# Strassen's products in layer 2, crossbar transposes and a new load order in a fused attention and MLP kernel

## The chip, the cores and the metric

The kernel runs on one core of a Trainium2 chip. The metric is device time in microseconds (us); every number for a kernel is the median of its executions unless it is called a range. A "span" is a little shorter than the time: it goes from the first to the last instruction of the one execution that was profiled. All readings of engines come from such profiles. PE is the matmul engine, DVE the vector engine, ACT the scalar engine, POOL is GpSimd, SP is the sync engine, which here issues nearly all DMAs, one after another (144 of 155 in the trace before).

## The reference

```python
# q, k, v: (8 batches, 8 heads, 576 rows, 64); w_ch1: (512, 2048); w_ch2: (2048, 512)
scores = scale * q @ k.T                      # window: 0 <= row - column < 64
attn = exp(scores - max) / (sum + 1e-9)       # masked
x = concat_heads(attn @ v)                    # (8, 576, 512)
xn = (x - mean) / sqrt(var + 1e-6) * g_ln     # layer norm (LN) of each row
out = x + relu(xn @ w_ch1) @ w_ch2            # float32
```

The kernel works in groups of 512 rows. Groups 0 to 7 are the first 512 rows of each batch; group 8 collects the last 64 rows of all eight batches, two batches to a block of 128; these four blocks are called tails. A group has four blocks of 128 rows.

## The kernel before

Each group is a list of units: sixteen units of layer 1 (four matmuls of 512 columns each), then sixteen of layer 2. Between the units of group g the kernel places, by slot number, the attention of batch g+1, the casts of batch g+2 and so on. Each engine gets its own instructions in this program order.

```python
    def l1(hc):                                    # layer 1: one unit
        ...
        for kc in range(NKC):                      # 4 matmuls of 512 columns
            nc.tensor.matmul(out=hps, lhsT=w1g[:, kc, 128*hc:128*(hc+1)], rhs=zT[g][:, kc, :], ...)
        nc.scalar.activation(out=hrT[:, hc, :], in_=hps, func=AF.Relu, ...)
    def l2(kb, part):                              # layer 2: one unit
        for hc in range(4*part, 4*part+4):         # 4 matmuls of 512 columns
            nc.tensor.matmul(out=ch[kb], lhsT=hrT[:, hc, 128*kb:128*(kb+1)], rhs=w2s[:, hc, :], ...)
        if part == 3: add_out(kb)                  # DVE: ch * rstd + x into osb, then the store
...
    def b_step(g, kb):                             # value matmuls, then on DVE: x, statistics, and
        nc.vector.scalar_tensor_tensor(out=z, in0=xn, scalar=mvg[...], in1=gB,   # z = (x - mean) * g
                                       op0=ALU.subtract, op1=ALU.mult)
    def zt_step(g, kb):                            # four PE transposes of z, one ACT copy into zT
...
        if g > 1 and b < B:                        # b = g + 1
            for j in range(4):
                at(1 + 6*j, s_mm, b, j); at(2 + 6*j, s_mask, b, j)
                at(7 + 6*j, b_step, b, j); at(min(13 + 6*j, 29), zt_step, b, j)
```

The softmax here doesn't subtract the row's maximum and nothing guards it: scores larger than these inputs give would overflow.

Of the kernel before, what the change touches and what calls it, by code (L numbers as in the profile page):

```python
# [20 lines left out]
def kernel(  # L21
# [10 lines left out]
    nc = tc.nc  # L32
# [8 lines left out]
    EPS = 1e-6  # L41
    scale = 1.0 / (D ** 0.5)
# [6 lines left out]
    p_pt = ctx.enter_context(tc.tile_pool(name="ppt", bufs=6))  # L49
    p_xn = ctx.enter_context(tc.tile_pool(name="pxn", bufs=8))  # L50
# [5 lines left out]
    ps_t = ctx.enter_context(tc.tile_pool(name="pst", bufs=2, space=PSUM))  # L56
# [7 lines left out]
    gB = p_const.tile([128, DM], FP32, tag="gB", name="gB")  # L64
    w1g = p_const.tile([128, NKC, HID], FP16, tag="w1g", name="w1g")
    w2s = p_const.tile([128, NHC, DM], FP16, tag="w2s", name="w2s")

# [20 lines left out]
    def load_tail(i):  # L88
        tq = p_in.tile([128, H, D], FP32, tag="tq32", name=f"tq32_{i}", bufs=1)
        tk = p_in.tile([128, 2, H, D], FP32, tag="qk32_1", name=f"tk32_{i}")  # L90
        tv = p_in.tile([128, 2, H, D], FP32, tag="qk32_0", name=f"tv32_{i}")
        tail32[i] = (tq, tk, tv)
        for r in range(2):
            b = 2 * i + r
            nc.sync.dma_start(out=tq[64 * r:64 * r + 64], in_=q[b, :, SM:S, :].rearrange("h s d -> s h d"))
            nc.sync.dma_start(out=tk[:, r], in_=k[b, :, S - 128:S, :].rearrange("h s d -> s h d"))
            nc.sync.dma_start(out=tv[:, r], in_=v[b, :, S - 128:S, :].rearrange("h s d -> s h d"))
# [13 lines left out]
    def cast_qk(b, half):  # L111
        for x in range(2):
# [60 lines left out]
    def w1_cast(i, eng):  # L173
        q2, pr = divmod(i, 2)
        t = wst.pop(("w1", i))
        dst = w1g[:, 2 * pr:2 * pr + 2, (HID // 4) * q2:(HID // 4) * (q2 + 1)]
        if eng == "act":
            nc.scalar.copy(out=dst, in_=t)
        else:
            nc.gpsimd.tensor_copy(out=dst, in_=t)  # L180
# [14 lines left out]

    def evac(x, out, in_):
# [5 lines left out]
    def t_main(b, x, half, eng=None):  # L202
        src = qk16.pop((b, x, half))
        j = 2 if b < 2 else 4
        tp = ps_t.tile([128, 8, 128], FP16, tag="tp", name=f"tp_{b}_{x}_{half}")
# [10 lines left out]
    def t_tail(i):  # L216
        q16, k16 = tail16.pop(i)
        tqk = (p_qkt.tile([128, NHP, 128], FP16, tag="tqT", name=f"tqT_{i}", bufs=1),
               p_qkt.tile([128, 2, NHP, 128], FP16, tag="tkT", name=f"tkT_{i}", bufs=1))
        tailT[i] = tqk  # L220
        tp = ps_t.tile([128, 2, NHP, 128], FP16, tag="tp", name=f"tpk_{i}")
        for r in range(2):
            for hp in range(NHP):
                nc.tensor.transpose(out=tp[:, r, hp, :], in_=k16[:, r, 2 * hp:2 * hp + 2, :], identity=ident16)
        evac(0, tqk[1], tp)
        tp = ps_t.tile([128, NHP, 128], FP16, tag="tp", name=f"tpq_{i}")
        for hp in range(NHP):
            nc.tensor.transpose(out=tp[:, hp, :], in_=q16[:, 2 * hp:2 * hp + 2, :], identity=ident16)
        evac(0, tqk[0], tp)

    def s_mm(g, j, pe_mask=False):
# [11 lines left out]
        for hp in range(NHP):  # L243
            for iw in range(2):
                for par in range(2):
# [4 lines left out]
                    else:  # L250
                        w = 2 * j + iw
                        lhsT = qkT[g][1][rows, hp, 64 * w:64 * w + 128]
                        rhs = qkT[g][0][rows, hp, 64 * w:64 * w + 64]
                    nc.tensor.matmul(out=sc[par][:, hp, iw, :], lhsT=lhsT, rhs=rhs,
                                     start=not pe_mask, stop=True, skip_group_check=pe_mask)
        for par in range(2):
            nc.scalar.activation(out=pt[:, par], in_=sc[par], func=AF.Exp, bias=0.0, scale=scale)
# [8 lines left out]
    def b_step(g, kb):  # L266
        kblk = f"{g}_{kb}"
        sfx, nb = ("r", 4) if g == NGRP - 1 else ("", None)
        xn = p_xn.tile([128, H, D], FP32, tag="xn" + sfx, name=f"xn_{kblk}", bufs=nb)
        x_norm[(g, kb)] = xn  # L270
# [17 lines left out]
        nc.vector.bn_stats(out=stats, in_=xn[:, :, :].rearrange("p h d -> p (h d)"))  # L288
        if g not in mvg:
            mvg[g] = p_grp.tile([128, 4, 2], FP32, tag="mvg" + sfx, name=f"mvg_{g}", bufs=1 if sfx else 2)  # L290
        nc.vector.bn_aggr(out=mvg[g][:, kb, :], in_=stats)
        z = p_blk.tile([128, DM], FP16, tag="z", name=f"z_{kblk}")
        zsd[(g, kb)] = z
        nc.vector.scalar_tensor_tensor(
            out=z, in0=xn[:, :, :].rearrange("p h d -> p (h d)"), scalar=mvg[g][:, kb, 0:1], in1=gB,
            op0=ALU.subtract, op1=ALU.mult,
        )

    def zt_step(g, kb, eng="act"):
# [4 lines left out]
        ztp = ps_t.tile([128, NKC, 128], FP16, tag="tp", name=f"ztp_{g}_{kb}")  # L304
# [8 lines left out]
    def group_stats(g, eng=nc.gpsimd):  # L313
        rstd[g] = p_grp.tile([128, 4], FP32, tag="rstdg", name=f"rstdg_{g}")
        rs = rstd[g]
        mv = mvg[g]
        tmp = p_grp.tile([128, 3, 4], FP32, tag="rstmp", name=f"rstmp_{g}")
        ve, hv, ab = tmp[:, 0], tmp[:, 1], tmp[:, 2]
        nc.vector.tensor_scalar(out=ve, in0=mv[:, :, 1], scalar1=EPS, scalar2=None, op0=ALU.add)
        nc.vector.tensor_scalar(  # L320
            out=ab.bitcast(I32), in0=ve.bitcast(I32), scalar1=1, scalar2=None,
            op0=ALU.logical_shift_right,
        )
        nc.vector.tensor_tensor(out=rs[:, :].bitcast(I32), in0=magt[:, :].bitcast(I32),  # L324
                                in1=ab.bitcast(I32), op=ALU.subtract)
        eng.tensor_scalar(out=hv, in0=mv[:, :, 1], scalar1=0.5, scalar2=0.5 * EPS,
                                op0=ALU.mult, op1=ALU.add)
# [6 lines left out]
    def mlp_units(g, split=0, two=False):  # L334
        hrT = p_hrt.tile([128, NHC, 512], FP16, tag="hrT", name=f"hrT_{g}")
        units = []
# [23 lines left out]
        def add_out(kb):  # L360
            o = p_blk.tile([128, DM], FP32, tag="osb", name=f"osb_{g}_{kb}")
            nc.vector.scalar_tensor_tensor(  # L362
                out=o, in0=ch[kb], scalar=rstd[g][:, kb:kb + 1],
                in1=x_norm[(g, kb)][:, :, :].rearrange("p h d -> p (h d)"), op0=ALU.mult, op1=ALU.add,
            )
            if g == NGRP - 1:
                for r in range(2):
                    nc.sync.dma_start(out=out[2 * kb + r, SM:S, :], in_=o[64 * r:64 * r + 64])
            else:
                nc.sync.dma_start(out=out[g, 128 * kb:128 * kb + 128, :], in_=o)  # L370
# [28 lines left out]
        for half in range(2):  # L399
            for i in range(split // 2):  # L400
                units.append(lambda half=half, i=i: l1_half(half, i))
        for hc in range(split, NHC):
# [4 lines left out]
        for kb in range(2 if two else 0, 4):  # L407
            for part in range(4):
                units.append(lambda kb=kb, part=part: l2(kb, part))
        return units  # L410
# [5 lines left out]
    ones1 = p_const.tile([1, 128], FP32, tag="ones1", name="ones1")  # L416
# [8 lines left out]
    nc.vector.memset(ones1, 1.0)  # L425
    nc.gpsimd.affine_select(
# [7 lines left out]
    nc.vector.tensor_scalar(out=mbias, in0=mask, scalar1=-1.0, scalar2=30000.0, op0=ALU.add, op1=ALU.mult)  # L434
    for b in range(2):
# [9 lines left out]
    for i in range(8):  # L445
        w1_cast(i, "pool")

    warm = ps_mm.tile([128, 512], FP32, tag="mm", name="warm")

    def keep_clock(n):  # L450
        m = mbias[:, :]
        mb = bass.AP(tensor=m.tensor, offset=m.offset, ap=[m.ap[0], [0, 8], m.ap[1]])
        for _ in range(n):
            nc.tensor.matmul(out=warm[:, :].rearrange("p (a i) -> p a i", i=64), lhsT=ident16, rhs=mb,  # L454
                             start=True, stop=True)


    keep_clock(4)
    gps = ps_mm.tile([128, DM], FP32, tag="mm", name="gps")
    nc.tensor.matmul(out=gps, lhsT=ones1, rhs=g1, start=True, stop=True)  # L460
    nc.vector.tensor_copy(out=gB, in_=gps)
# [51 lines left out]
    for g in range(NGRP):  # L513
        units = mlp_units(g, (8, 16)[g] if g < 2 else 0, g == 0)
# [6 lines left out]
        if g == 0:  # L521
# [3 lines left out]
            at(4, group_stats, 0, nc.vector)  # L525
# [6 lines left out]
            at(16, s_mm, 1, 0, True)  # L532
            at(17, s_mm, 1, 1, True)
# [9 lines left out]
            at(29, s_mm, 1, 2, True)  # L543
            at(30, s_mm, 1, 3, True)
            at(30, load_v, 2, 0, 4)
            at(31, b_step, 1, 2)
        if g == 1:
# [3 lines left out]
            at(2, zt_step, 1, 2)  # L551
            at(5, zt_step, 1, 3)
# [8 lines left out]
            for c in range(4):  # L561
                at(7, vB_cur, 2, c, 1)
                if c < 3:
                    at(7, vB_prev, 2, c, 1)
            for j in range(4):
                at(9 + 4 * j, s_mm, 2, j)
                at(10 + 4 * j, s_mask, 2, j)
                at(13 + 4 * j, b_step, 2, j)
                at(17 + 4 * j, zt_step, 2, j)
        if g > 1 and b < B:  # L570
            at(0, alloc_vB, b)
            at(0, make_vB, b)
            for j in range(4):
                at(1 + 6 * j, s_mm, b, j)
                at(2 + 6 * j, s_mask, b, j)
                at(7 + 6 * j, b_step, b, j)
                at(min(13 + 6 * j, 29), zt_step, b, j)
        if g > 0:
            at(13, group_stats, g)
        for n, i in enumerate(TAILS.get(g, ())):  # L580
            at(3 + 12 * n, t_tail, i)
            at(5 + 12 * n, s_mm, NGRP - 1, i)
            at(6 + 12 * n, s_mask, NGRP - 1, i)
            at(10 + 12 * n, b_step, NGRP - 1, i)
            at(16 + 12 * n, zt_step, NGRP - 1, i)
        if 0 < g and b + 1 < B:
# [56 lines left out]
```

## Time and profile before

| | before |
|---|---|
| time, median of 4 | 336.12 us (335.85 to 336.39) |
| profiled span | 334.6 us |
| PE busy | 96% |
| DVE, ACT, POOL busy | 50%, 52%, 34% |
| DMA, the hardware queue's share of 16 engines | 54.1% |

From the page of the kernel before: engine totals, then four of the lines that cut the span into 40 slices (digits are the busy tenths of a slice; PEclk is the granted matmul clock in tenths of full speed), and the engine shares of the chain that ended last.

```profile
PE 322.8 (96%) x2887; PEld 171.9 (51%) x2887; DVE 168.0 (50%) x307; ACT 175.5 (52%) x292; POOL 114.8 (34%) x198
PE   7988999999999999999999999999999999999994
POOL 7577655413800195008400780058004103201000
PEclk9999999999999999999999999999999999999999
DMA  8999999976239557950369188903460155020022
PE 85%; DVE 4%; SPq 4%; DMA 2%; ACT 1%; issue 1%; POOL 1%; ACTq 0%
```

PE is busy for 80% or more of every slice from the second to the last but one, the clock row shows no reduction, and the last chain is PE work. So PE work that goes away is time that goes away, as long as nothing else makes PE wait. The waits of PE, longest first (total, times, longest one):

```profile
PE warm L454 <- DVE mbias L434: 2.3, 1, 2.3
PE hph_1_0_574 L377 <- ACT zT_375 L309: 0.9, 1, 0.9
PE hph_0_1_1011 L377 <- ACT hrT_992 L382: 0.7, 1, 0.7
```

A busy PE is not the price of a matmul, because matmuls overlap: in this trace one of 512 columns in layer 2 lasts 380 ns. The distance from one matmul's start to the next is: 216 ns at 512 columns, 109 ns at 256, 56 ns for a 128-column transpose.

### The profile page before, as it was taken

Reading aid. Unit: us, or ns where it says so; the run is one execution under the profiler, and the core shown is the slowest. Engines: PE = TensorE matmul, PEld = TensorE weight load, DVE = VectorE, ACT = ScalarE, POOL = GpSimd, SP = SyncE. Lnnn points to the kernel's source line nnn. Section 1 sums busy time; section 2 is a strip of 40 time slices with the busy share of each in tenths; the row PEclk is TensorE's granted clock in tenths of the full one; section 3 lists DMA queues with packets and bytes.
Section 4 is the critical chain, followed back from the end, with each engine's and each line's share of the span. In section 5 each row is a group of like instructions: output and inputs, shape, how many; then the busy total and the mean of one; then the engine's idle time right before and its main releaser. Section 6 shows DMA issues by size and latency. Waiting matters only on the chain.

```text
span 334.6 us, 6996 instructions
## 1 busy us (share of the span) xinstructions
PE 322.8 (96%) x2887; PEld 171.9 (51%) x2887; DVE 168.0 (50%) x307; ACT 175.5 (52%) x292; POOL 114.8 (34%) x198
## 2 busy tenths in 40 slices
PE   7988999999999999999999999999999999999994
PEld 2556445786554455545545554456445444444441
DVE  1795682777933565286415751767235714241011
ACT  2586515485267644974468356763675157505500
POOL 7577655413800195008400780058004103201000
PEclk9999999999999999999999999999999999999999
DMA  8999999976239557950369188903460155020022
GB/s 194 284 385 258 355 265 297 256 232 123 62 105 309 103 104 187 309 103 34 118 212 216 29 199 255 219 23 97 118 104 2 65 149 72 16 82 33 0 63 63
DMA packets 85410, 51.02 MB, mean 152 GB/s; under 512 B 55713, under 2 KB 76193, under 8 KB 85378
## 3 DMA queue, kind: packets, MB, share of 16 engines
q1 hardware_dynamic: 84736, 48.24, 54.1%
q0 software_dynamic: 640, 2.33, 3.1%
q8 instruction: 22, 0.36, 0.5%
q14 instruction: 10, 0.08, 0.1%
q10 hardware_dynamic: 2, 0.00, 0.0%
HBM read 38.80 MB, written 9.44 MB: 144 GB/s over the span
## 4 chain that ended last, share of the span: by engine, by line
PE 85%; DVE 4%; SPq 4%; DMA 2%; ACT 1%; issue 1%; POOL 1%; ACTq 0%
DMA w1s_126<-in_moe_w_ch_dram 2%; SPq L130 2%; SPq L78 1%; PE ch_2_852 L353 1%; PE ch_2_3635 L353 1%; PE ch_1_4056 L353 1%; PE ch_1_3588 L353 1%; PE ch_2_3076 L353 1%; PE ch_2_2587 L353 1%; PE ch_1_1979 L353 1%; PE ch_1_4421 L353 1%; PE ch_2_4077 L353 1%; PE ch_1_3029 L353 1%; PE ch_1_2540 L353 1%; PE ch_2_2026 L353 1%
## 5 line engine op out<-in xcount | busy, mean ns | idle before, releaser
L341 PEld LDWEIGHTS <-w1g 128*128 128x128 f16 x480 | 44.9, 98 | 53.0 <-issue 2.9
L377 PEld LDWEIGHTS <-w1g 128*128 128x128 f16 x192 | 18.1, 98 | 5.4 <-issue 2.1
L454 PE MATMUL warm<-mbias,ident_99 128*128 128x512 f16 x21 | 8.1, 491 | 2.3 <-DVE mbias L434 2.3
L353 PEld LDWEIGHTS <-hrT_4513 128*128 128x128 f16 x64 | 6.3, 98 | 7.5
L353 PEld LDWEIGHTS <-hrT_3733 128*128 128x128 f16 x64 | 6.0, 98 | 7.0
L353 PEld LDWEIGHTS <-hrT_2685 128*128 128x128 f16 x64 | 6.0, 98 | 6.5
L353 PEld LDWEIGHTS <-hrT_4162 128*128 128x128 f16 x64 | 6.0, 98 | 6.5
L353 PEld LDWEIGHTS <-hrT_1635 128*128 128x128 f16 x64 | 5.9, 97 | 6.5
L353 PEld LDWEIGHTS <-hrT_992 128*128 128x128 f16 x64 | 5.9, 98 | 6.3
L353 PEld LDWEIGHTS <-hrT_2131 128*128 128x128 f16 x64 | 5.9, 98 | 6.3
L353 PEld LDWEIGHTS <-hrT_3181 128*128 128x128 f16 x64 | 5.9, 98 | 6.3
L362 DVE SCALAR_TENSOR_TENSOR osb_0_4641<-ch_0_4624,rstdg_4598,xn_0_2321 128x512 f32<-128x512 f32 x1 | 0.8, 752 | 16.2 <-PE ch_0_4624 L353 16.2
L329 POOL TENSOR_TENSOR rstmp_1863<-rstdg_1862 128x4 f32<-128x4 f32 x2 | 0.8, 386 | 22.5 <-DVE rstdg_1862 L324 22.4
L329 POOL TENSOR_TENSOR rstmp_2913<-rstdg_2912 128x4 f32<-128x4 f32 x2 | 0.8, 386 | 21.2 <-DVE rstdg_2912 L324 21.2
L329 POOL TENSOR_TENSOR rstmp_3948<-rstdg_3947 128x4 f32<-128x4 f32 x2 | 0.8, 386 | 21.2 <-DVE rstdg_3947 L324 21.2
L329 POOL TENSOR_TENSOR rstmp_2426<-rstdg_2425 128x4 f32<-128x4 f32 x2 | 0.8, 388 | 20.6 <-DVE rstdg_2425 L324 20.6
L329 POOL TENSOR_TENSOR rstmp_3475<-rstdg_3474 128x4 f32<-128x4 f32 x2 | 0.8, 388 | 19.7 <-DVE rstdg_3474 L324 19.6
L106 POOL MEMSET vt_4312<- 128x16 f16 x1 | 0.2, 168 | 21.0 <-PE xps_2_4279 L280 21.0
L309 ACT COPY zT_2461<-ztp_3_4492 128x512 f16<-128x512 f16 x1 | 0.6, 587 | 9.2 <-PE ztp_3_4492 L306 9.2
L392 PE MATMUL ch_0_700<-w2s,hrT_495 128*128 128x512 f16 x16 | 4.8, 381 | 0.1
L180 POOL CAST w1g<-w2s 128x1024 f16<-128x1024 f32 x4 | 4.6, 1157 | 1.0 <-DMA w2s<-in_moe_w_ch_dram 1.0
L454 PEld LDWEIGHTS <-ident_99 128*128 128x128 f16 x21 | 2.1, 118 | 5.1 <-issue 3.4
(1267 smaller groups left out, 918.2 us busy)
## 6 DMA issues: line engine op xcount, KB each, us to landing
w2s<-in_moe_w_ch_dram SPq DMA_DIRECT2D x4, 512.0 KB, 10.6
v_0_110<-in_v_dram SPq DMA_DIRECT2D x4, 256.0 KB, 6.1
v_1_442<-in_v_dram SPq DMA_DIRECT2D x4, 256.0 KB, 7.7
v_2_950<-in_v_dram SPq DMA_DIRECT2D x4, 256.0 KB, 7.4
v_3_1339<-in_v_dram SPq DMA_DIRECT2D x4, 256.0 KB, 4.3
v_4_1785<-in_v_dram SPq DMA_DIRECT2D x4, 256.0 KB, 8.4
v_5_2348<-in_v_dram SPq DMA_DIRECT2D x4, 256.0 KB, 6.7
v_6_2835<-in_v_dram SPq DMA_DIRECT2D x4, 256.0 KB, 6.9
```

The lines of the kernel that those rows point to most:

```text
L78: nc.sync.dma_start(out=t[:, :].rearrange("p (h m) -> p h m", h=H), in_=src[b, :, 256 * half:256 * half + 256, :].rearrange("h (p j) d -> ...
L106: nc.gpsimd.memset(vt[:, :, :, D:D + 1], 1.0)
L130: nc.sync.dma_start(out=v32[b][:, c], in_=v[b, :, 128 * c:128 * c + 128, :].rearrange("h s d -> s h d"),)
L180: nc.gpsimd.tensor_copy(out=dst, in_=t)
L309: nc.scalar.copy(out=dst, in_=ztp)
L329: eng.tensor_tensor(out=ab, in0=rs, in1=rs, op=ALU.mult)
L341: nc.tensor.matmul(out=hps, lhsT=w1g[:, kc, 128 * hc:128 * (hc + 1)], rhs=zT[g][:, kc, :], start=(kc == 0), stop=(kc == NKC - 1),)
L353: nc.tensor.matmul(out=ch[kb], lhsT=hrT[:, hc, 128 * kb:128 * (kb + 1)], rhs=w2s[:, hc, :], start=(hc == 0), stop=(hc == NHC - 1),)
L362: nc.vector.scalar_tensor_tensor(out=o, in0=ch[kb], scalar=rstd[g][:, kb:kb + 1], in1=x_norm[(g, kb)][:, :, :].rearrange("p h d -> p (h d) ...
L377: nc.tensor.matmul(out=hps[:, e], lhsT=w1g[:, kc, 128 * hc:128 * (hc + 1)], rhs=zT[g][:, kc, 256 * half:256 * half + 256], start=(kc == 0) ...
L392: nc.tensor.matmul(out=ch[kb], lhsT=hrT[:, hc, 128 * kb:128 * (kb + 1)], rhs=w2s[:, hc, :], start=(hc == 0), stop=(hc == NHC - 1),)
L454: nc.tensor.matmul(out=warm[:, :].rearrange("p (a i) -> p a i", i=64), lhsT=ident16, rhs=mb, start=True, stop=True)
```

## The change

The intent is to take work off PE. Layer 2 of groups 2 to 8 becomes Strassen's seven block products: the activations are four blocks, the second weight is four blocks, and seven products of half size replace eight, at the price of sums of blocks (DVE) and more additions out of PSUM (DVE). For that, the rows must be fully normalised before layer 1, because a factor per row can no longer be applied to a sum of row blocks at the end; this moves the making of z from DVE to POOL. The transposes of q, of the LN rows and of most tails go from PE to the DMA crossbar (DMAs that SP issues and that write a block transposed). The loads of a batch are issued behind the stores of the group.

```diff
+    def z_step(g, kb):                     # groups 2 to 8: on POOL, in four operations
+        nc.gpsimd.tensor_scalar(out=ve, in0=var, scalar1=1.0, scalar2=EPS, op0=ALU.mult, op1=ALU.add)
+        nc.gpsimd.tensor_tensor(out=rs, in0=ve, in1=mhalf, op=ALU.pow)
+        nc.gpsimd.tensor_scalar(out=nm, in0=mu, scalar1=rs, scalar2=-1.0, op0=ALU.mult, op1=ALU.mult)
+        nc.gpsimd.tensor_scalar(out=z, in0=xv, scalar1=rs, scalar2=nm, op0=ALU.mult, op1=ALU.add)
     def zt_step(g, kb):
+        if XZ <= g < NGRP - 1:             # XZ = 2
+            nc.sync.dma_start_transpose(out=zT[g][:, :, 128 * kb:128 * kb + 128], in_=z)
+            return
 ...
+    def product(n, p):                     # one half of one of the seven products: 8 matmuls of 256 columns
+        which, a, wv = {1: ("A", hv[:, :, 0, 0:256], w2v[:, :, 0, 0, :]),
+                        ...
+                        6: ("A", sS[2], wT[2]), 5: ("C", sS[1], w2v[:, :, 0, 1, :]), ...}[n]
+        for c in range(NHC // 2):
+            nc.tensor.matmul(out=bank[which][:, p, :], lhsT=a[:, c, 128*p:128*p+128], rhs=wv[:, c, :], ...)
+    def post(which, kb0, f):               # DVE: x += bank, seven times a group
+        nc.vector.tensor_tensor(out=xv, in0=bank[which], in1=xv, op=ALU.add)
 ...
         if g == 1:
+            at(13, cast_qk, 3, 0);  at(17, cast_qk, 3, 1)           # POOL
+            at(18, cast_v, 3, 0, 2); at(18, cast_v, 3, 2, 4)        # POOL
+            at(19, alloc_vB, 3);    at(19, make_vB, 3)              # POOL issues two copies
+            at((13, 17, 20, 23)[j], b_step, 2, j)                   # and z_step, POOL
+            at((18, 21, 25, 28)[j], zt_step, 2, j)
 ...
+        for n, i in enumerate(TAILS.get(g, ())):                    # tail i in group g
+            at(ts[2], z_step, NGRP - 1, i)                          # ts[2] is 9 for the first
+        if len(TAILS.get(g, ())) == 2:                              # group 7
+            at(9, cast_tail, TAILS[g][1])                           # stands behind that z
+            at(12, t_tail, TAILS[g][1], 0)                          # PE transposes
+        if n + 1 < B:
+            at(40, load_qk, n + 1, 0); ...                          # last slot: behind the stores
```

(The gain g is folded into the first weight by scaling its casts, batch 1 gets its mask on DVE instead of PE, and result rows are built in place.)

## The prediction

> **What bounds it now.** TensorE. The page gives PE 322.8 of 334.6 us busy, DVE 50%, ACT 52%, POOL 34%; the chain that ended last is 85% PE; the table of windows has PE busy 20.00 of 20 us from 100 to 280 us. The granted clock is 1.00. Start-to-start spacings of matmuls in the trace are the price of PE work: 216 ns at 512 columns, 109 ns at 256, 56 ns for a 128-column transpose, about 0.35 us for a block's sixteen score matmuls, 0.40 us for its value matmuls.
>
> **What leaves PE.**
> 1. Layer 2, groups 2 to 8: 64 matmuls of 512 columns (13.8 us a group) become 112 of 256 (12.2 us): 1.6 us x 7 = 11.3 us.
> 2. PE transposes fall from 448 to 236: LN rows 7 to 8 us (a quartet occupied about 0.35 us), q 4.8 us, tails 2 us.
> 3. Eight 512-column mask matmuls of batch 1: 1.7 us.
> Sum about 27 us, all on the critical path. A sum by group (about 30 us instead of 34 in groups 2 to 5) gives about 309 us without a new stall.
>
> **What is added.** DVE: four sums of 2048 f16 elements per group; the 1024-element f16 mask multiply takes 0.68 to 0.84 us in the trace, so 6 to 7 us; seven additions from PSUM at 0.69 us instead of four at 0.75, +1.8 us; z (0.87 us each) leaves. That is about 21 us of a 30 us group, 24 with a tail, and nearly full in group 1, with its weight sums. POOL: z with its root, some 6 us a group estimated from its casts (1.04 us per 1024 elements); the W1 casts become scalings in two pieces, which I expect at nearly cast speed. DMA: about 6.7 MB of crossbar transposes. [...] A batch's loads took about 15 us (99.6 to 114.1) and now start at the group's end.
>
> **New stalls.** (a) Group 1 to 2: the last LN block goes through a crowded DVE, POOL and a DMA issued four units (3.5 us) before use: 1 to 2 us. (b) Batch 1's scores now wait for a DVE mask: about 1 us. (c) In groups with tails the sums or PSUM additions may come late for the third product: below 1 us each. (d) Groups 2 and 4 carry batch and tail loads ahead of the transposes on one queue; should hold by 2 to 4 us. Together 2 to 3 us.
>
> **Predicted: 311 us, range 305 to 321.** Faster by over 2%: 0.94; within 2%: 0.04; slower: 0.02.
>
> **What would show it.** Right: PE still 95% busy or more; groups 3 to 5 start 29.5 to 31.5 us apart; 256-column matmuls of layer 2 spaced 109 ns; DMA transposes landing in 2 to 4 us; PE waits below 12 us. Wrong: PE waiting at a group's first layer-1 matmul on a transpose (DMA step); at the third or seventh product on DVE (DVE step); first layer-1 matmul well after 20.4 us, or layer 2 of group 0 waiting on weight casts (POOL step).
>
> **What would make it wrong.** Crossbar transposes several times slower than plain DMAs, or blocking the queue ahead of loads and stores (up to 5 us in each of six groups); POOL scaling at half the cast's speed (3 to 5 us at the start)[...].

About 336 us less about 27 us of PE work is 309, and 2 to 3 us of new stalls make 311. Stall (a) has a transpose on its way, so its 1 to 2 us are an estimate that no trace backed.

## The result, and the profile after

The changed kernel took **328.3 us** (328.02 to 329.02, 4 runs) against 336.12 us. The ratio is 0.976, with a 95% interval of 0.972 to 0.980. Ratios here are the mean time of one kernel's fast runs over that of the other's of the same rounds, so not quite the ratio of the medians. Executions over 1.5% slower than the fastest of the same kernel are left out of the means. The kernel is faster by 2.4%; the predicted 311 us would have been 7.5%, and 328.3 lies outside the predicted range of 305 to 321.

The page after, the lines that answer to those of before:

```profile
PE 303.1 (93%) x3009; PEld 193.2 (59%) x3009; DVE 206.7 (63%) x392; ACT 150.1 (46%) x252; POOL 165.7 (51%) x251
PE   7989989999976999999999998999999995999993
POOL 6588665513990598269816891597145307020000
PEclk9999999999997999999999999999999997799999
DMA  8999999976748994998199999962951680003013
PE 59%; DMA 14%; POOL 11%; DVE 6%; SPq 6%; issue 3%; ACT 1%; POOLq 0%; ACTq 0%
```

PE's row has holes at slices 12, 13 and 34 that were not there, and the clock row falls to 7 at 13, 34 and 35. The share of PE in the last chain fell from 85% to 59%; DMA and POOL took its place. The waits of PE after:

```profile
PE hps L392 <- DMA zT<-z: 7.0, 2, 5.1
PE tpq L245 <- POOL tq L118: 3.6, 1, 3.6
PE warm L593 <- DVE mbias L586: 2.3, 1, 2.3
```

Two new waits stand at the top, 10.6 us together. They are three places in time. In the next fence, PE around each (start, length, what; in brackets the idle time before it and what ended it), cut to the lines on either side of the gap:

```profile
95.41 0.41 PE L283 MATMUL sc<-qkT,qkT 64*128 64x64 f16 x16
100.88 3.48 PE L392 MATMUL hps<-zT,w1g 128*128 128x512 f16 x9 [5.06 <-DMA zT<-z]
...
193.68 1.92 PE L464 MATMUL pC<-w2s,sS 128*128 128x256 f16 x16
197.58 2.78 PE L392 MATMUL hps<-zT,w1g 128*128 128x512 f16 x12 [1.98 <-DMA zT<-z]
...
268.81 2.76 PE L392 MATMUL hps<-zT,w1g 128*128 128x512 f16 x12
275.19 0.61 PE L245 MATMUL tpq<-ident,tq 128*128 128x128 f16 x4 [3.62 <-POOL tq L118]
```

The first is the start of group 2, the second the start of group 5, the third the middle of group 7. After the first and third, matmuls of 512 columns started 427 ns apart instead of 216. The table of windows shows the clock of those stretches (columns: window, its length, then busy time and count of PE, PEld, DVE, ACT and POOL, the granted clock, the DMA share and GB/s):

```profile
98.00:104.00 6.00, 3.12 (x9) 1.14 (x10) 0.00 (x0) 0.60 (x1) 0.30 (x1) 0.72 0.74 219
104.00:134.00 30.00, 30.00 (x320) 20.08 (x319) 23.34 (x42) 15.30 (x26) 21.18 (x31) 1.00 0.98 183
274.00:281.00 7.00, 5.81 (x26) 3.21 (x27) 0.05 (x1) 3.09 (x5) 3.11 (x5) 0.53 0.00 0
```

The clock record is halved (0.50) from 100.3 to 103.7 us and from 274.4 to 281.2 us, which is 3.4 and 6.8 us. When it was halved, PE had stood idle since 95.8 and 271.6 us; when it came back, PE had worked again for 2.8 and 6.0 us. There is no half-rate matmul behind the gap of 2.0 us. The two long gaps thus cost more than their own length.

The time by groups, in us, from the first layer-1 matmul of a group to that of the next (the last column is the mended kernel of the fifth experiment, in a fast run):

| group | before | after | mended |
|---|---|---|---|
| (start-up) | 20.4 | 21.0 | 20.0 |
| 0 | 39.1 | 38.3 | 40.1 |
| 1 | 38.7 | 41.6 | 38.6 |
| 2 | 34.0 | 31.7 | 30.4 |
| 3 | 35.7 | 32.5 | 32.5 |
| 4 | 34.0 | 32.5 | 30.4 |
| 5 | 35.7 | 32.5 | 32.5 |
| 6 | 32.2 | 29.0 | 29.0 |
| 7 | 31.8 | 36.0 | 30.1 |
| 8, to its last matmul | 27.9 | 26.2 | 26.2 |
| (after the last matmul) | 5.0 | 5.5 | 5.4 |

A wait at the start of group n counts in the row of group n-1. Groups 3, 5, 6 and 8, which have no large gap inside, are 1.7 to 3.2 us shorter. Groups 1 and 7 became longer.

What stands behind the first gap is seen on POOL. First the line of DVE that ends the statistics of the third block, then POOL's timeline after, in group 1 (z of the third and fourth block of group 2 is the L342 to L345 sequence, twice; vB is a second copy of v, which POOL makes by issuing DMAs):

```profile
86.23 0.18 DVE L328 BATCH_NORM_AGGREGATE mvg<-stats 128x2 f32<-128x6 f32 x1
...
85.34 2.55 POOL L128 CAST qk<-qk 128x1024 f16<-128x1024 f32 x2
87.83 0.24 POOL L135 MEMSET vA<- 128x32 f16 x1
87.91 2.88 POOL L147 CAST vA<-v 128x1024 f16<-128x1024 f32 x2
90.72 0.52 POOL L151 MEMSET vB<- 64x520 f16 x1
91.19 0.74 POOL L165 DMA_DIRECT2D vB<-vA  x1
91.94 0.55 POOL L166 DMA_DIRECT2D vB<-vA  x1
92.57 0.32 POOL L342 TENSOR_SCALAR rsz<-mvg 128x1 f32<-128x1 f32 x1
...
94.86 0.77 POOL L345 TENSOR_SCALAR z<-xn,rsz 128x512 f16<-128x512 f32 x1
95.71 0.19 POOL L342 TENSOR_SCALAR rsz<-mvg 128x1 f32<-128x1 f32 x1
...
97.01 1.30 POOL L345 TENSOR_SCALAR z<-xn,rsz 128x512 f16<-128x512 f32 x1
```

DVE had the statistics of the third block ready at 86.41 us (its `mvg` ends there), but POOL, in order, first cast batch 3 and issued its copies, and came to that block at 92.57. The fourth block followed and ended at 98.31; its transpose was issued at 98.33 and landed at 100.74; group 2 started at 100.88. The line of the wait names DMA, because the transpose landed last. The third block lost 6.2 us in POOL's queue (86.41 to 92.57), and the fourth stood behind it.

The second gap is of another kind. The fourth z of group 5 ended at 189.70 us, its transpose was issued at 192.23 and landed at 197.44: it was 2.5 us late to be issued and then took 5.2 us to land. The third gap is again POOL's order. The cast of q of the fourth tail, for which PE waits, stands behind the z of the third tail, and that z waits for DVE:

```profile
270.90 0.54 POOL L342 TENSOR_SCALAR rsz<-mvg 128x1 f32<-128x1 f32 x1 [14.94 <-DVE mvg L328]
...
273.16 1.37 POOL L345 TENSOR_SCALAR z<-xn,rsz 128x512 f16<-128x512 f32 x1
274.48 0.16 POOL L117 MEMSET vt<- 128x16 f16 x1
274.54 0.60 POOL L118 CAST tq<-tq 128x512 f16<-128x512 f32 x1
```

How the transposes themselves did (SP instructions and landing times of all 24 LN transposes):

```profile
L353 SPq DMA_TRANSPOSE zT<-z x24: 1189/1202/2048, 80.7 to 253.3; - x24
DMA to landing us min/median/max: 2.4/2.5/5.7
```

They move 128 KB each; the stores of 128 KB in this trace took 2.5 us as well (median of 3). The transposes of q, of 256 KB, took 3.7 us (median of 10) where stores of 256 KB took 2.7.

### The profile page after: what moved, and what is told of

Same layout as the page of the kernel before. It is cut to its first block, busy times and chain, and to the rows that moved or that the text cites. A ratio compares the mean times of both kernels' runs of the same rounds, so it can differ in the third digit from the quotient of the medians.

```text
span 326.8 us, 7417 instructions
## 1 busy us (share of the span) xinstructions
PE 303.1 (93%) x3009; PEld 193.2 (59%) x3009; DVE 206.7 (63%) x392; ACT 150.1 (46%) x252; POOL 165.7 (51%) x251
## 4 chain that ended last, share of the span: by engine, by line
PE 59%; DMA 14%; POOL 11%; DVE 6%; SPq 6%; issue 3%; ACT 1%; POOLq 0%; ACTq 0%
PE hps L392 23%; PE pA L464 9%; PE pC L464 7%; PE pB L464 6%; PE hph L513 4%; DMA qk<-in_q_dram 4%; SPq L141 4%; DMA zT<-z 4%; DMA w2s<-in_moe_w_ch_dram 3%; POOL qk L128 3%; PE ch L404 3%; PE xps L317 2%; PE sc L283 2%; PE tp L226 2%; DMA w1s<-in_moe_w_ch_dram 2%
## 5 line engine op out<-in xcount | busy, mean ns | idle before, releaser
L392 PE MATMUL hps<-zT,w1g 128*128 128x512 f16 x480 | 113.9, 388 | 7.0 <-DMA zT<-z 7.0
L396 ACT ACTIVATE hrT<-hps 128x512 f16<-128x512 f32 x120 | 71.8, 598 | 61.8 <-PE hps L392 52.4
L342 POOL TENSOR_SCALAR rsz<-mvg 128x1 f32<-128x1 f32 x28 | 11.2, 402 | 95.4 <-DVE mvg L328 94.8
L290 ACT ACTIVATE pt<-sc 128x512 f16<-128x512 f32 x72 | 39.0, 595 | 32.1 <-DVE xn L471 18.3
L464 PEld LDWEIGHTS <-sS 128*128 128x128 f16 x448 | 43.2, 98 | 5.3
L128 POOL CAST qk<-qk 128x1024 f16<-128x1024 f32 x32 | 36.2, 1147 | 9.2 <-DMA qk<-in_q_dram 4.7
L464 PEld LDWEIGHTS <-hrT 128*128 128x128 f16 x336 | 32.5, 98 | 5.1
L297 DVE TENSOR_TENSOR pt<-pt,mask 128x1024 f16<-128x1024 f16 x32 | 26.8, 839 | 11.3 <-ACT pt L290 11.2
L464 PE MATMUL pA<-wT,sS 128*128 128x256 f16 x224 | 26.9, 273 | 0.0
L464 PE MATMUL pC<-w2s,sS 128*128 128x256 f16 x224 | 26.8, 273 | 0.0
L345 POOL TENSOR_SCALAR z<-xn,rsz 128x512 f16<-128x512 f32 x28 | 25.2, 900 | 2.9
```

The source lines that it names most:

```text
L128: nc.gpsimd.tensor_copy(out=dst[:, :].rearrange("p (a j) e d -> p a e j d", j=j), in_=t[:, :].rearrange("p (a e j d) -> p a e j d", e=2, j ...
L290: nc.scalar.activation(out=o, in_=i, func=AF.Exp, bias=0.0, scale=scale)
L297: nc.vector.tensor_tensor(out=ptv, in0=ptv, in1=mb, op=ALU.mult)
L345: nc.gpsimd.tensor_scalar(out=z, in0=xv, scalar1=rs, scalar2=nm, op0=ALU.mult, op1=ALU.add)
L392: nc.tensor.matmul(out=hps, lhsT=w1g[:, kc, 128 * hc:128 * (hc + 1)], rhs=zT[g][:, kc, :], start=(kc == 0), stop=(kc == NKC - 1),)
L464: nc.tensor.matmul(out=bank[which][:, p, :], lhsT=a[:, c, 128 * p:128 * p + 128], rhs=wv[:, c, :], start=(first and p == 0 and c == 0), st ...
```

## The experiments

The theory after reading the traces: the PE work fell as predicted, and about 14 us were lost in three stalls that come from the order of work in queues (POOL twice, the DMA queue once), two of them made longer by the clock. The main rival: crossbar transposes are slow, or DMA is too full, as the name in the longest wait suggests. Experiments start from the changed kernel; "mended" ones start from the fifth. The kernel before ran 7 times beside each set, with medians of 336.4, 337.0 and 336.6 us; the three sets (1 to 4; 5, 7, 8 and the first form of 6; 9 and the second form of 6) ran on three different chips, so a difference across sets is less sure by some tenths of a us. Line numbers in experiment kernels are shifted where lines were added.

### 1. Cast the fourth tail earlier (x1_tail)

```diff
-            at(9, cast_tail, TAILS[g][1])
+            at(7, cast_tail, TAILS[g][1], "qk")   # q and k only
+            at(9, cast_tail, TAILS[g][1], "v")
```

> Only change to the changed kernel: in group 7 GpSimd casts q and k of the fourth tail two slots earlier, ahead of the z of the third tail; its v cast stays behind. Theory (GpSimd's in-order queue): the 3.78 us PE gap in group 7 before tpq, and the half-rate stretch of matmuls after it (about 2.4 us at 427 ns spacing), both go: 328.3 to about 322 us (321 to 323.5). Rival (the tail's loads, issued late in group 6, come too late): the gap stays above 2 us and the time above 326 us.

Measured: 323.39 us (322.14 to 324.07), 0.961 of before. The wait for `tq` is gone from PE's list, group 7 fell from 36.0 to 30.1 us, and no half-rate matmul is left in it. The time is inside the theory's range, but it fell by only 4.9 us: in this profile the clock behind the gap at the start of group 2 stayed halved for 6.8 us instead of 3.4, and group 2 took 32.9 us instead of 31.7. The loads had landed in time all along. In the changed kernel's trace those of q and k had landed by 265.0 us and the cast of q began at 274.5. In this run's profile POOL waited for nothing but them and cast q and k at once, while the z that used to stand in front of them came 7 us later:

```profile
264.25 0.62 POOL L122 CAST tq<-tq 128x512 f16<-128x512 f32 x1 [7.93 <-DMA tq<-in_q_dram]
265.45 1.04 POOL L123 CAST tk<-tk 128x1024 f16<-128x1024 f32 x1 [0.58 <-DMA tk<-in_k_dram]
271.25 0.54 POOL L355 TENSOR_SCALAR rsz<-mvg 128x1 f32<-128x1 f32 x1 [4.77 <-DVE mvg L341]
```

The rival for this gap, late loads, falls. The order on POOL was worth 5.9 us in group 7 for a wait of 3.6 us: the rest is the halved clock (0.53 granted from 274 to 281 us in the changed kernel).

### 2. Casts of batch 3 on ACT (x2_cast3act)

```diff
-            at(17, cast_qk, 3, 1)
-            at(18, cast_v, 3, 0, 2)
-            at(18, cast_v, 3, 2, 4)
-            at(19, alloc_vB, 3)
-            at(19, make_vB, 3)
+            at(17, cast_qk, 3, 1, (0, 1), True)   # True: nc.scalar.copy
+            at(18, cast_v, 3, 0, 2, True)
+            at(18, cast_v, 3, 2, 4, True)
+            at(23, alloc_vB, 3)
+            at(23, make_vB, 3)
```

> Only change to the changed kernel: four casts of batch 3 in group 1 (q and k of the second half, v) go from GpSimd to ScalarE, and the vB copies of batch 3 are issued after the last z of group 2. The crossbar transposes stay. Theory (z of the last two blocks of group 2 waits in GpSimd's queue behind 7 us of casts and copies): the 5.2 us gap of PE at the start of group 2 shrinks to 0.5 to 2 us and its 1.3 us of half-rate matmuls goes: about 323 us (322 to 324.5). Rival (crossbar transposes or a crowded DMA are slow): the gap stays above 4 us and the time above 327 us.

Measured: fast runs 321.45, 322.03 and 322.90 us, 0.957 of before; a fourth run, which was the profiled one, was slow (327.37 us), with other gaps that a fast run need not have, so the profile is not used for them. The gap itself is read in the mended kernel below, which has the same edit in a fast run: 2.0 us instead of 5.1, without a half-rate stretch. The crossbar transposes and their queue were untouched, so the larger part of the gap was POOL's queue.

### 3. LN rows of group 2 transposed on PE (x3_pez2)

```diff
-    XZ = 2
+    XZ = 3
```

> Only change to the changed kernel: the LN rows of group 2 are transposed on PE again, z still on GpSimd. Theory (GpSimd's queue, not the crossbar): PE now waits for the same z tiles inside layer 2 of group 1 instead, 4 to 5 us in all, and group 2 starts no earlier than 100 us; with 1.2 us more PE work the time is 327.5 to 330.5 us. Rival (crossbar transposes are what is slow): the wait goes and the time falls to 322 to 324 us.

Measured: 326.87 us; fast runs 325.17 to 327.06, 0.970 of before. This is a little better than the range the theory gave (the missing gap named below is worth about 2 us), and above the rival's. The wait did not go, it moved: PE now waits for z itself, inside layer 2 of group 1.

```profile
PE ztp L357 <- POOL z L345: 4.0, 1, 4.0
PE tpq L245 <- POOL tq L118: 3.6, 1, 3.6
```

Group 2 started at 102.2 us instead of 100.9. The crossbar was not what made PE wait there. In this run the gap at the start of group 5 was missing too, although nothing was changed there; I supposed that this gap depends on how loads and stores happen to meet, which the next experiment was to test.

### 4. Loads of the second tail in group 3 (x5_tailload)

```diff
+        if g == 3:
+            at(22, load_tail, 1)
...
-                at(1, load_tail, i)
+                if g != 4:
+                    at(1, load_tail, i)
```

> Only change to the changed kernel: the loads of the second tail go from slot 1 of group 4, where they sit in the same queue between the loads of batch 6 and the transposes, to slot 22 of group 3. Theory (group 4's DMA queue is full, so its transposes come late): the 2.1 us PE gap at the start of group 5 goes, about 326.3 us (325.6 to 327). Rival (the last transpose is late because the vB copies run beside it, or because SP issues transposes at 1.3 us each): the gap stays above 1.5 us, 327.8 us or more.

Measured: 328.58 and 332.94 us in the fast runs, 335.4 in two slow ones; against before 0.983, unclear. A miss: the expected 326.3 us did not come. The profiled run is a slow one, so its reading is a lead only (the 332.94 us run has the same granted clock, 0.967, as the slow ones, so it probably holds for that run too). In it the gap at the start of group 5 is gone, but the tail's loads now ran ahead of the stores of group 3, and DVE waited for a store to leave a buffer of x:

```profile
177.18 0.69 DVE L323 TENSOR_TENSOR xn<-xps,rcp 128x512 f32<-128x512 f32 x1 [6.27 <-DMA out_dram<-xn]
```

PE then waited 4.0 us for a DVE mask behind it. If this holds for the fast runs, it is the reason why the change puts loads behind stores: x is built, added to and stored in one buffer, and a late store holds up DVE one group later.

### 5. All three orders mended (x6_all)

The edits of 1 and 2, and the second tail's loads at slot 17 of group 3, ahead of its last transposes and copies, so that they are done before the stores.

```diff
+        if g == 3:
+            at(17, load_tail, 1)      # instead of slot 22; the rest as in 1, 2 and 4
```

> The changed kernel with three orders mended: q and k of the fourth tail cast earlier in group 7 (first experiment), four casts of batch 3 on ScalarE (second), and the second tail's loads at slot 17 of group 3, ahead of group 3's last transposes and vB copies rather than beside them. Theory (the missing time is three stalls made by queue order, and the PE work left as predicted): 6 + 5.5 + 2 us come back, 314.5 us (312.5 to 317); no PE gap above 2.5 us. Rival (DMA has no room, so a stall taken away here comes back elsewhere, as it did when those loads were moved to slot 22): 318 us or more, with a new PE gap above 3 us.

Measured: **316.75 us**; fast runs 316.28 to 316.88 and one slow run of 322.42; 0.939 of before. This lies in the range of the theory and outside the rival's. PE's waits in the fast profile:

```profile
PE warm L606 <- DVE mbias L599: 2.3, 1, 2.3
PE hps L405 <- DVE pt L310: 2.0, 1, 2.0
PE ch L541 <- POOL w2s L214: 1.5, 1, 1.5
```

The second is what is left at the start of group 2. DVE is named because a mask ended at the same moment (98.5 us), but layer 1 does not read it. The last z was ready at 95.2 us, and its transpose was issued at once and landed at 98.5, 3.3 us later. Group 5 starts without a wait, groups 2 and 4 take 30.4 us, and there is no half-rate stretch between start-up and the end. The rows of the table above add up: 3.1 + 1.3 + 2.2 + 5.9 us came back in groups 1, 2, 4 and 7, and 0.9 us was lost before group 1 (a wait for weight casts in group 0 that varies from run to run: 0.5 us in the profile after, 1.5 here, 0.3 in experiments 7 and 8), together 11.6 us of span.

What the third edit is worth by itself is not shown. By the means of the fast runs (328.4, 323.3 and 322.1 us) the first edit alone took off 5.2 us and the second alone 6.3, together 11.4; all three took off 11.8. And the gap at the start of group 5 was missing in experiment 3 too, without this edit.

### 6. The mended kernel without Strassen (x7_all_noseven, x11_noseven_ok)

```diff
-        units, s_sums = mlp_units(g, (8, 16)[g] if g < 2 else 0, g == 0, g > 1)
+        units, s_sums = mlp_units(g, (8, 16)[g] if g < 2 else 0, g == 0, g == NGRP - 1)
...
-        if g > 1:                      # s_sums, the shared transpose bank
+        if g == NGRP - 1:
```

> The mended kernel with Strassen's products taken out of groups 2 to 7 (plain layer 2, 64 matmuls of 512 columns; the last group keeps them). Theory (Strassen is worth its matmul spacings, 1.6 us a group, when PE is fed): 9.7 us slower than the mended kernel run beside it (8 to 11), PE groups 3 and 5 some 1.6 us longer. Rival (its sums and additions on DVE eat the gain): within 5 us of the mended kernel.

The first form took 325.31 us (fast runs 323.10 to 327.14) but its result was wrong by a relative error of 0.42: one of the weight sums overwrites a block of the second weight in group 2, and plain layer 2 still reads that block. It was run again with that sum moved to the last group:

```diff
-        if g == 2:
+        if g == NGRP - 1:
             at(3, w2_sums, 1, 0, 4)
             at(4, w2_sums, 1, 4, 8)
```

> Again the mended kernel without Strassen in groups 2 to 7, now correct: the sum that overwrites a block of the second weight moves to the last group (the earlier run gave a wrong result because plain layer 2 read the overwritten block). Theory: Strassen is worth 1.6 us a group where PE is fed, less where its group had a stall to hide: 7 to 10 us slower than the mended kernel's 316.75 us, so 324 to 327 us. Rival (its sums on DVE eat the gain): below 321 us.

Measured, and correct: 324.6 us (322.68 to 326.53), 0.964 of before, 7.9 us more than the mended kernel. In its profile groups 4 and 6, which have no wait inside, are 1.6 and 1.7 us longer than in the mended kernel, as the spacings say, and groups 2 to 7 together 9.2 us; start-up and group 0, where the mended kernel's profile has its wait for weight casts, are 1.8 us shorter. Strassen is worth nearly what the sum of matmul spacings gave; its sums on DVE did not eat it.

### 7. The mended kernel with transposes on PE (x10_all_pe)

```diff
-    XQ = 3
-    XZ = 2
+    XQ = 99
+    XZ = 99
```

> The mended kernel with the LN rows of groups 2 to 7 and q of batches 3 to 7 transposed on PE again (tails stay on the crossbar). Theory (each PE transpose costs its occupancy, 0.3 us a quartet of LN rows and 56 ns for q): 11 to 13 us slower than the mended kernel. Rival (the crossbar's load on DMA and its landing times cost about what PE saves): within 4 us of it.

Measured: 325.43 us (324.63 to 326.45), 0.965 of before, 8.7 us more than the mended kernel. The step is between the two theories but near the first: groups 2 to 5 are 1.6 to 1.8 us longer each. In the profile groups 1 to 7 are 9.9 us longer (start-up and group 0 are 2.3 us shorter), and PE's waits there are about the same, 3.5 us in the mended kernel and 3.6 here. So 9.9 us is the work, and that is the 176 transposes at their spacing of 56 ns. The expectation was too high because it priced a quartet (the four transposes of one LN block) at 0.3 us. From its first start to the next instruction a quartet took 0.22 us here; before it took 0.32 where value matmuls came next and 0.22 elsewhere.

### 8. z in three operations (x9_all_three)

```diff
-        nc.gpsimd.tensor_scalar(out=nm, in0=mu, scalar1=rs, scalar2=-1.0, op0=ALU.mult, op1=ALU.mult)
-        nc.gpsimd.tensor_scalar(out=z, in0=xv, scalar1=rs, scalar2=nm, op0=ALU.mult, op1=ALU.add)
+        nc.gpsimd.tensor_scalar(out=z, in0=xv, scalar1=mu, scalar2=rs, op0=ALU.subtract, op1=ALU.mult)
```

> The mended kernel with z on GpSimd in three operations instead of four (subtract the mean and multiply by the root in the one pass over the row, so the small negated-mean product, 409 ns a block, goes). Theory (GpSimd's chain to z sets what is left at the start of group 2): the remaining gap there shrinks by 0.4 to 1.5 us and the time by 0.5 to 2 us against the mended kernel. Rival (what is left there is the transposes' landing): same within 0.4 us.

Measured: 326.28 us (325.90 to 326.93), 9.5 us *slower* than the mended kernel. Neither theory held. The groups of instructions on POOL, with and without the edit (busy us, mean ns of one):

```profile
L357 POOL TENSOR_SCALAR z<-xn,mvg,rsz 128x512 f16<-128x512 f32 x28 | 63.8, 2278 | 3.0
```

against the mended kernel's

```profile
L358 POOL TENSOR_SCALAR z<-xn,rsz 128x512 f16<-128x512 f32 x28 | 24.9, 889 | 2.9
```

The same shape costs 2278 ns as subtract-then-multiply and 889 ns as multiply-then-add. Saving one small operation made the row pass 2.6 times as long. The edit also takes the two scalars from two tiles (mvg and rsz) instead of one, so which of the two makes the pass slow is not shown. It was not intended, but it is a strong test of the theory: 28 x (2278 - 889) ns less 28 x 415 ns is 27 us more work on POOL, an engine busy half of the time, and the kernel lost 9.5 us.

### 9. Three more slots (x12_best2)

```diff
-                at(22 + 3 * m, w2_sums, i, 0, 4)
-                at(23 + 3 * m, w2_sums, i, 4, 8)
+                at(24 + 3 * m, w2_sums, i, 0, 4)
+                at(25 + 3 * m, w2_sums, i, 4, 8)
...
-            ts = (15, 16, 19, 24) if n else (4, 5, 9, 14)
+            ts = (15, 16, 19, 24) if n else (4, 5, 9, 16)
...
-            for i, (x, half) in zip((13, 17, 13, 21) if ...
+            for i, (x, half) in zip((13, 18, 13, 22) if ...
```

> The mended kernel with three slots shifted: the weight sums of group 1 two slots later so that the last LN block of group 2 passes DVE first, PE's transposes of k one slot later, the third tail's LN transposes two slots later. Theory (the gaps that are left, 2.1 us at the start of group 2, twice 0.65 us before transposes of k, 0.8 us in group 7, are queue order too): 1.5 to 3.5 us faster than the mended kernel, 313.3 to 315.3 us. Rival (they are the floor of the chain from value matmuls over DVE, GpSimd and crossbar to layer 1): 316 us or more.

Measured: 315.53 us, but the four fast runs are 313.61, 314.07, 316.99 and 317.00: two values, not a spread. It is the fastest kernel by its median, 0.935 of before, but its gain over the mended kernel (316.28 to 316.88) is inconclusive. The profiled run was one of 317 us. In it the gap at the start of group 2 is 1.3 us and that of group 7 is gone, so those were order; the two gaps before the transposes of k in groups 3 and 5 came back as waits of 0.6 us for DVE at the third product; and a gap of 2.7 us stands at the start of group 4, on a transpose that shares the DMA queue with the loads moved in experiment 5. Whether that gap is what separates 314 from 317 us is not shown.

## Why the prediction was wrong, point by point

- **PE is the bound, and PE work that leaves is time.** Right. Groups 2 to 8 took 231.4 us before and 211.1 in the mended kernel; with the 1.6 us of small waits in the latter set aside, about 22 us of work left. The prediction's 27 us over all groups contained about 3.8 us in groups 0 and 1 (1.7 for masks, the rest transposes of batches 2 and 3), so 23 was meant for these. Strassen: 7.9 us by the times and 9.2 by the groups of the profile, where 9.7 was the sum for six groups (experiment 6). LN rows and q: 8.7 us by the times and 9.9 by the groups, where about 12 was the sum (experiment 7).
- **"DMA transposes landing in 2 to 4 us."** Right for the LN rows by the median, 2.5 us (2.4 to 5.7), as against 2.5 us for a store of the same 128 KB in the same trace. The transposes of q took 3.7 us, a third more than stores of their size (2.7 us).
- **"New stalls ... Together 2 to 3 us."** This is the step that failed. The measured stalls and their consequences came to about 14.3 us in the profile after: 5.1 us of waiting at the start of group 2 and 1.3 us of halved clock, 2.0 us at the start of group 5, and 5.9 us in group 7 with its halved clock. That is about 12 of the 17.3 us by which 328.3 missed 311. The other 5, by the table: without these stalls groups 2 to 8 are 20.2 us shorter than before where 23 was meant, start-up with groups 0 and 1 is 2.4 us shorter where 3.8 was meant, and the end after the last matmul is 0.5 us longer. Three things were missed in the term:
  - (a), the way of the last LN blocks of group 2, was named but put at 1 to 2 us. I counted each engine's share of busy time and the length of the chain, not what stands in front of it in POOL's queue: 7.2 us of casts and copies of batch 3 between the second and third z (85.34 to 92.57). Experiments 2 and 3 show it.
  - Group 7 was not named at all. The cast of the fourth tail was placed in the same slot as, and behind, a z that cannot start before DVE has its statistics: POOL stood idle for 14.9 us before that z, and the cast came behind it, at 274.54 us. Experiment 1 shows it.
  - The halved clock was not in the sum. At 0.50 from 274.4 to 281.2 us, it turned a wait of 3.6 us into a loss of 5.9 us.
- **POOL: "z with its root, some 6 us a group".** Mis-sized. The four operations of one block are 402 + 690 + 409 + 900 = 2401 ns, so 9.6 us a group. I estimated them from casts, which are one long pass; the three small operations on a single column cost more than the row. Their times also vary: z took 0.77 us at 236.9 us, with DVE idle, and 1.37 us at 273.2 us, beside DVE's block sums, but 0.77 us again at 204.4, beside a mask multiply. That DVE's work stretches POOL's is thus not shown.
- **(d) Groups 2 and 4 carry loads ahead of the transposes; "should hold by 2 to 4 us".** Half right: group 2 held, group 4 did not, by 2.0 us. There the last transpose was 2.5 us late to be issued and took 5.2 us to land. Experiment 5, which moves a tail's loads away, has no such gap, but neither has experiment 3, which left them; so that these loads are the cause is argued and not shown. Experiment 4 shows that moving them to the wrong place does not help.
- **(b) and (c), masks of batch 1 and late sums.** PE's list of waits after has none for a mask of batch 1, and none for a sum or an addition at a product. They cost less than was allowed for them.
- **Signs named.** "PE still 95% busy or more" failed (93%), and so did "groups 3 to 5 start 29.5 to 31.5 us apart" (32.5) and "PE waits below 12 us" (17.6 in the list of waits, 2.3 of them at the start). The spacing of 109 ns held. "PE waiting at a group's first layer-1 matmul on a transpose (DMA step)" came true, but at group 2 the step that it was to accuse was the wrong one: the transpose was fast (2.4 us) and was issued late. At group 5 it was late and slow.

The 316.75 us of the mended kernel and the predicted 311 still differ. Its profile has 2.0 us at the start of group 2, 1.5 us on weight casts in group 0, twice 0.5 us before transposes of k and 0.6 us in group 7: 5.1 us of waits beyond the start-up. Without them it would stand near 311.6 us (an estimate from these waits), where the prediction's sum without a new stall was 309; so the sum of work was itself too high, by some 2 to 3 us.

## What to carry to other kernels

When work moves to an engine that is half idle, the question is not its busy share but its queue: look for what stands in front of the moved work at the moment when it becomes ready, and whether something that waits has been placed ahead of something that PE needs. A wait that names a DMA has to be followed one step further back, to when the DMA could have been issued. And on the matmul engine keep every single gap well below 3 us, going by these runs: after start-up, gaps up to 2.7 us (experiment 9, whose granted clock was 1.00 from 98 to 168 us) were followed by no half-rate stretch, and gaps of 3.1 us (experiment 8), 3.6 and 5.1 us (the changed kernel) were. The 5.1 and 3.6 us gaps of the changed kernel cost their length and then 1.3 and 2.3 us more.

## What else these runs measured

- A pass over a row on POOL with two per-partition scalars, 128x512 f32 to f16, took 889 to 900 ns as multiply-then-add with both scalars in one tile and 2278 ns as subtract-then-multiply with the scalars in two tiles (means of 28 each).
- In the changed kernel, on POOL, a two-step scalar operation on a single column, 128x1, took 192 to 1107 ns (mean 405, 56 of them), and a power of 128x1 549 to 894 ns (mean 690), where a pass over 512 elements took 900.
- A transpose on the DMA crossbar cost the issuing engine, in the changed kernel, 1.2 us of SP for each 128-row LN transpose (median of 24), where a plain 256 KB store took 0.44 us. With six to eight transposes a group, that is SP time that the loads and stores behind them have to share.
- In experiment 8 a PE wait of 3.1 us (its spacing 3.3 us) was followed by 3.4 us at a granted clock of 0.5; the mean over that run's span was 0.993, against 0.996 in the mended kernel.
